# A PSUM bank of its own for gate and lists, and float16 expert products from the third set on

## The chip, the cores and the metric

The kernel runs on one core of a Trainium2 chip. TensorE multiplies, VectorE, ScalarE and GpSimd work on tiles in SBUF and PSUM, SyncE (SP) issues most DMAs. The metric is the device time of one launch in microseconds; lower is better. TensorE's operands may be float32 read in a reduced form (fp32r) or float16; a product of full accuracy is made of three such products of high and low parts.

## The reference

Two layers follow each other. The first is a filter in the frequency domain over 8 batches of 2496 tokens with 256 channels, the second a mixture of 8 experts with two chosen per token, over all 19968 tokens:

```
X = rfft(x, axis=1);  y = irfft(X * (filt_r + 1j * filt_i), n=2496, axis=1)
x = y.reshape(19968, 256)
noisy = x @ w_gate + log1p(exp(x @ w_noise)) * noise
top2 = two largest of noisy per token;  g = softmax over these two
out[token] += g[k] * (relu(x[token] @ w1[e]) @ w2[e])     # for both k, e = top2[k]
```

w1 is 8 x 256 x 1024, w2 is 8 x 1024 x 256.

## The kernel before, in words

**Two streams in one program.** The transform of batch after batch (`fft_stream`) is cut into small steps: `s1`, `kg1`, `kg2`, `t3`, `i2` are matrix products with small tables, each followed by an eviction from PSUM by ScalarE or VectorE. The expert (`expert`) is a generator that yields after each piece of a token block. `run` draws transform steps between the expert's pieces, as many as `PACE` asks for. Each engine executes its instructions in the order in which they stand.

**Sets and blocks.** When a batch is transformed and its tokens are assigned, the tokens that fill whole blocks of 512 for one expert become the next set. Sets 0 and 1 have 2 and 10 blocks, sets 2 and 3 six each, sets 4 to 7 ten each; singles and half blocks follow. In the code `ready` is the set's number plus one. A block takes 13 expert steps: 8 hidden tiles f (relu of x by w1: six products of 512 columns each), one step for the next block's front, and 4 output tiles (h by w2: 24 products of 256 columns each). A hidden tile is evicted twice, by ScalarE (`hh`, line 1371) and VectorE (`hl`, line 1372); an output tile is scaled by the gate on ScalarE (line 1398) and added to the output by an indirect DMA of GpSimd.

**Number formats.** Where `ready >= HALF` the weights, x and the hidden tiles are split into float16 pairs, scaled by powers of two (`wsplit`, `turn`, `pair`); before that they are fp32r pairs. The scales need the largest values. `wscales` finds them in 88 steps (`NPREP`): 64 loads of 256 KB of weights (`wp`, line 598), each squared with accumulation on ScalarE (line 603), then 12 loads of y with a maximum on VectorE (line 620), and two `powers` steps. A load is issued two steps ahead of its square. `run` spreads the steps so that they end after `READY` expert steps:

```
while not self.scaled and state["due"] * READY < NPREP * state["y"]:
    state["due"] += 1
    next(self.preps)
```

For later batches `xscale` makes a scale from the maxima that `i2` leaves in `ymax`.

**Gate and lists.** At the end of a batch's transform `logit_sum`, `logits` and `gating` put the logits into a PSUM tile `lg`; `gate` is a chain of small VectorE instructions to the two chosen experts (`oh`), their weights (`dense`) and, with the products `rk`, each token's place in its expert's list. `slots` (`sl`, `st`) makes the table of blocks. `route` writes the lists: one-hot tiles `oc` on VectorE (lines 1060 to 1062), products `ra` (line 1065), a transpose, and an indirect DMA. `i2` copies `dense` behind the rows of the odd half (line 549) before these go to DRAM.

**PSUM.** Eight banks: "hps" 2 (hidden), "yps" 2 (outputs), "xps" 1 and "fps" 3. After the start all tiles that are asked for by `ps` come from "fps": the transform's and those of gate, slots and lists. Every third hidden tile uses "xps" from set 1 on (`by_dma`), and "yps" in set 0.

Of the kernel before, what the change touches and what calls it, by code (L numbers as in the profile page):

```python
# [24 lines left out]
NG = 22  # L25
# [110 lines left out]
RAW = 3  # L136
HALF = 5
EVERY = 3
# [7 lines left out]
TINY = 2.0 ** -60  # L146
EARLY = {"q1": "hps", "q2": "hps", "q5": "yps", "q6": "yps", "u1": "xps", "u3": "yps"}
BANKS = {"hps": 2, "yps": 2, "xps": 1, "fps": 3}

# [3 lines left out]
class Moe:  # L153
# [40 lines left out]
    def setup(self):  # L194
# [36 lines left out]
        self.tab = cp.tile([1, 2, SW], F32, name="tab")  # L231
        self.ymax = cp.tile([128, 2 * NB, 6], F32, name="ymax")
        self.xm = cp.tile([128, 1], F32, name="xm")
        self.wmax = cp.tile([128, 2 * E], F32, name="wmax")
# [78 lines left out]
    def ps(self, nm):  # L313

        tag = self.banks.get(nm, "fps") if self.early else "fps"
        return self.PS.tile([128, 512], F32, tag=tag, name=nm, bufs=BANKS[tag])

# [205 lines left out]
    def i2(self, n, g0):  # L523
        nc, P, h = self.nc, self.P, n % 2
        Dh, Dl = self.cD
        th, tl = self.t3t.pop((n, g0))
        k = min(4, NG - g0)
        m = 128 * k
        p = self.ps("q6")
        if tl is None:  # L530
            nc.tensor.matmul(p[:RP, :m], self.rD, th[:120, :m], start=True, stop=True)
        else:
            nc.tensor.matmul(p[:RP, :m], Dh, th[:120, :m], start=True, stop=False)
            nc.tensor.matmul(p[:RP, :m], Dh, tl[:120, :m], start=False, stop=False)
            nc.tensor.matmul(p[:RP, :m], Dl, th[:120, :m], start=False, stop=True)  # L535
        w = 128 + E * h
        if n == 0:
            yt = P.tile([RP, 4, 128], F32, name="yt", tag=("mxl0", "mxh1", "mxl1")[g0 // 4 % 3], bufs=1)
        else:
            yt = P.tile([RP, 4, 128 + E], F32, name="yt", bufs=2)  # L540
        e = nc.scalar.copy(yt.bitcast(U16)[:, :k, :256].rearrange("p g (two d) -> p g two d", two=2),  # L541
                       p.bitcast(U16)[:RP, :2 * m].rearrange("p (g d two) -> p g two d", g=k, two=2))
        if n == 2:
            self.yev.append(e)
        if n >= 2 * FIRSTS:
            nc.vector.tensor_reduce(self.ymax[:RP, n, g0 // 4:g0 // 4 + 1], yt.bitcast(U16)[:, :k, 128:256].bitcast(BF16),
                                    axis=AX.XY, op=ALU.max, apply_absolute_value=True)
        if h:
            nc.scalar.copy(yt[:, :k, 128:], self.dense[:, g0:g0 + k])
        y = self.y[BLK + n // 2 * ROWS:BLK + (n // 2 + 1) * ROWS].rearrange("(p g) d -> p g d", p=RP)  # L550
        nc.sync.dma_start(y[:, g0:g0 + k, h * 128:h * 128 + w], yt.bitcast(I32)[:, :k, :w])
# [26 lines left out]
    def xscale(self, bt):  # L578

        nc = self.nc  # L580
        if not self.known:
            self.owed.append(bt)
            return
        nc.vector.tensor_reduce(self.xm, self.ymax[:, :2 * bt + 2], axis=AX.XY, op=ALU.max)
        q = yield from self.powers(self.xm, 1, TX)
        t = self.xs[bt + 1] = self.cp.tile([128, 2], F32, name=f"xs{bt}")
        nc.vector.tensor_copy(t, q[:, :, 0])
        yield
# [270 lines left out]
    def gate(self, bt, lgp):  # L859
# [11 lines left out]
        u, w, l, z = A[:, 17:], B[:, 16:], t("gl"), t("gz")  # L871
        nc.scalar.activation(u, lg[:, :, 8:16], AF.Exp)

        v.tensor_scalar_add(w, u, 1.0)
# [9 lines left out]
        nz = t("gz")  # L884
        v.tensor_add(nz, l, lg[:, :, 0:8])
        keyb = self.key[:RP].unsqueeze(1).to_broadcast(sh)
# [5 lines left out]
        for i in range(2):  # L892
            mi, ci = t(f"m{i}", [RP, NG]), t(f"c{i}", [RP, NG])
            oi = P.tile(sh, F32, name=f"oh{i}", tag=("gl", "oh1")[i], bufs=1)
# [28 lines left out]
        v.tensor_mul(nz, oh[1], bc(e2))  # L923
        v.tensor_add(self.dense, self.dense, nz)
        yield None
        q = self.ps("rk")
        nc.tensor.matmul(q[:RP, 0:8], self.tri[:RP, :RP], rs, start=True, stop=True)
        nc.tensor.matmul(q[:, 8:16], self.ones[:RP, :128], rs, start=True, stop=True)
        nc.tensor.matmul(q[:E, 16:17], rs, self.ones[:RP, 0:1], start=True, stop=True)


# [4 lines left out]
        v.scalar_tensor_tensor(mm, hb, -float(LR), self.base, op0=ALU.mult, op1=ALU.add)  # L936
        v.scalar_tensor_tensor(rw, mm, float(LR - 1), q[:, 8:16], op0=ALU.add, op1=ALU.add)
        v.tensor_single_scalar(rw, rw, 7, op=ALU.arith_shift_right)
# [6 lines left out]
        v.scalar_tensor_tensor(mm, beg, float(LR), mm, op0=ALU.mult, op1=ALU.add)  # L945
        rb = t("rb", [RP, E])
        v.tensor_add(rb, q[:RP, 0:8], mm[:RP])
        v.tensor_add(src, src, rb.unsqueeze(1).to_broadcast(sh))
# [21 lines left out]
        v.tensor_scalar_add(rf, ri, -float(BLK + bt * ROWS + ROWS // 2))  # L970
        v.tensor_add(self.base, self.base, q[:, 8:16])
        v.tensor_add(self.cnt, self.cnt, q[:E, 16:17])
        yield hi, lo, row, rf
# [59 lines left out]
    def route(self, bt, hi, lo, row, rf):  # L1033
# [10 lines left out]
        lr, tv = self.half[:RP, :4 * LR].rearrange("p (l j) -> p l j", j=4), self.half[:RP, 4 * LR:]  # L1044
        for g0 in range(0, NG, 4):
            q = self.ps("ra")[:, :HR]
            for g in range(g0, min(g0 + 4, NG), 2):
                t = P.tile([128, 1024], F16, name="oc", tag=("xh", "xl", "b")[g // 2 % 3], bufs=1)


                ol, vv = t[:RP, 0:4 * LR], t[:RP, 4 * LR:4 * LR + 4 * HR]
                if bt < 2:
                    ol, vv = (a.rearrange("p (l j) -> p l j", j=4) for a in (ol, vv))
                else:
                    ol, vv = (a.rearrange("p (j l) -> p l j", j=4) for a in (ol, vv))

                def w(a):
                    return a if bt < 2 else a.rearrange("p l j -> p j l")

                v.tensor_tensor(w(vv), w(lr[:, :HR]), w(bc(hi[:, g:g + 2], HR)), op=ALU.is_equal)  # L1060
                v.tensor_mul(w(vv), w(vv), w(tv[:, 2 * g:2 * g + 4].unsqueeze(1).to_broadcast([RP, HR, 4])))
                v.tensor_tensor(w(ol), w(lr), w(bc(lo[:, g:g + 2], LR)), op=ALU.is_equal)
                for j in range(4):
                    n = RP if g + j // 2 < NG - 1 else QA
                    nc.tensor.matmul(q, ol[:n, :, j], vv[:n, :, j], start=(g == g0 and j == 0), stop=(j == 3 and g + 2 >= min(g0 + 4, NG)))
            if g0 == 0:
# [8 lines left out]

        o = P.tile([HR, LR], F32, name="ro", **(dict(tag="th", bufs=3) if bt < 2 else dict(tag="ut1", bufs=1)))
        v.tensor_single_scalar(o, q, 0.0, op=ALU.not_equal)
# [256 lines left out]
    def expert(self, parts, may, fill=None):  # L1334
# [5 lines left out]
        while self.ahead:  # L1340
# [10 lines left out]
            if not self.ahead or self.ahead[0][3] or sum(len(a[2][0]) for a in self.ahead) < 4:  # L1351
                self.fetch(may)
            third = ("xps", 1) if self.by_dma(ent) else ("yps", 2)
            hh = []
# [172 lines left out]
```

## Time and profile before

| what | before |
|---|---|
| median of 3 runs | 2177.8 us (2176.26 to 2184.05) |
| the profiled execution | 2164.38 us, span 2162.5 us |
| granted TensorE clock, mean | 0.991 |
| TensorE busy | 2095.9 us, 14517 matmuls |
| VectorE busy | 1466.3 us |
| ScalarE busy | 1286.1 us |
| DMA | 428.48 MB, 198 GB/s over the span |

The span is the time from the first to the last instruction of one profiled execution. A busy matmul is a pipelined one: the durations of neighbours overlap, and what a product costs is the step from its start to the next start. Set 0 begins its first block near 142 us, set 1 at 221, set 2 at 517, set 3 at 693, set 4 at 868.

### The profile page before, as it was taken

The numbers are of one execution on the slowest core, as the hardware profiler recorded it, in microseconds if no ns is written. First come the engines' busy times: TensorE is split into PE (matmuls) and PEld (weight loads), VectorE is DVE, ScalarE is ACT, GpSimd is POOL, SyncE is SP. The second block draws the span as 40 slices with busy tenths as digits, with TensorE's granted clock in tenths as the row PEclk, the third lists the DMA queues.
The fourth block names the chain that finished last, engine by engine and source line by source line (L and its number), as shares of the span: only waits on it lengthen the run. The fifth ranks groups of instructions, "written<-read, shape, count | busy, mean of one in ns | idle before, by whom it ended". The sixth has DMA issues, their size and how long they took to land. (4 is left out here: it accounts for less than half of the span.)

```text
span 2162.5 us, 42794 instructions
## 1 busy us (share of the span) xinstructions
PE 2095.9 (97%) x14517; PEld 1595.5 (74%) x14517; DVE 1466.3 (68%) x3221; ACT 1286.1 (59%) x2505; POOL 1029.2 (48%) x946
## 2 busy tenths in 40 slices
PE   8779999999999999999999999999999999999997
PEld 6447988888888888766766676666666666667886
DVE  5866779877978886678665986589666664333443
ACT  6666866786577446656664565555566564333443
POOL 4233334434544344445444453555655665654563
PEclk9989999999999999999999999999999999999999
DMA  9588989999999775767766687666889999869997
GB/s 255 165 259 223 222 223 215 252 228 228 223 214 233 161 156 137 178 150 183 155 156 131 152 182 165 146 121 132 233 210 240 240 249 234 170 142 229 276 280 175
DMA packets 511673, 428.48 MB, mean 198 GB/s; under 512 B 215679, under 2 KB 397015, under 8 KB 511447
## 3 DMA queue, kind: packets, MB, share of 16 engines
q1 hardware_dynamic: 450135, 341.27, 60.2%
q0 software_dynamic: 61312, 84.40, 23.1%
q8 instruction: 116, 1.90, 0.4%
q14 instruction: 110, 0.90, 0.1%
HBM read 263.92 MB, written 122.03 MB: 178 GB/s over the span
## 5 line engine op out<-in xcount | busy, mean ns | idle before, releaser
L1372 DVE SCALAR_TENSOR_TENSOR hl<-hps,hh 128x512 f16<-128x512 f32 (+3 forms) x712 | 432.4, 623 | 356.6 <-ACT hh L1371 354.7
L1399 POOL DMA_INDIRECT out<-stage,ids x316 | 532.9, 1686 | 270.4 <-ACT stage L1398 167.0
L1158 POOL DMA_INDIRECT stage<-y,ids x316 | 347.9, 1101 | 535.7 <-DMA xt<-stage 433.9
L124 PE MATMUL yps<-w,hh 128*128 128x256 f16 (+1 forms) x2048 | 556.5, 278 | 5.2 <-ACT stage L1398 3.4
L125 PE MATMUL yps<-w,hh 128*128 128x256 f16 (+1 forms) x2048 | 551.2, 277 | 0.0
L126 PE MATMUL yps<-w,hl 128*128 128x256 f16 (+1 forms) x2048 | 541.9, 277 | 1.8 <-DVE hl L1372 1.5
L1371 ACT ACTIVATE hh<-hps 128x512 f16<-128x512 f32 (+3 forms) x712 | 376.7, 550 | 198.9 <-PE hps L126 183.8
L125 PE MATMUL hps<-mxl,w1h 128*128 128x512 f16 (+1 forms) x1024 | 394.4, 386 | 2.2 <-DVE mxl L1246 1.3
L126 PE MATMUL hps<-mxh,w1l 128*128 128x512 f16 (+1 forms) x1024 | 394.0, 386 | 0.0
L124 PE MATMUL hps<-mxh,w1h 128*128 128x512 f16 (+1 forms) x1024 | 385.6, 388 | 5.1 <-DVE hl L1372 5.1
L1398 ACT ACTIVATE stage<-yps,gt 128x256 f32<-128x256 f32 x316 | 143.1, 475 | 329.0 <-PE yps L126 202.0
L124 PEld LDWEIGHTS <-hh 128*128 128x128 f16 x1760 | 172.2, 98 | 52.4 <-issue 6.2
L126 PEld LDWEIGHTS <-hl 128*128 128x128 f16 x1760 | 171.5, 98 | 47.9 <-DVE hl L1372 1.9
L125 PEld LDWEIGHTS <-hh 128*128 128x128 f16 x1760 | 172.2, 98 | 34.2 <-issue 2.6
L124 PEld LDWEIGHTS yps<-w,hh 128*128 128x128 f32 x768 | 145.8, 190 | 12.5 <-ACT stage L1398 2.2
L126 PEld LDWEIGHTS yps<-w,hl 128*128 128x128 f32 x768 | 145.0, 190 | 10.3 <-issue 1.7
L125 PEld LDWEIGHTS yps<-w,hh 128*128 128x128 f32 x768 | 145.4, 191 | 4.6
L126 PEld LDWEIGHTS <-w1l 128*128 128x128 f16 x640 | 62.6, 98 | 71.8 <-issue 1.5
L541 ACT COPY yt<-q 117x1024 uint16<-117x1024 uint16 x96 | 90.9, 947 | 40.7 <-PE q L535 32.1
L1228 DVE COPY stage<-xt 128x1024 uint16<-128x1024 uint16 (+2 forms) x174 | 109.0, 679 | 1.4 <-DMA xt<-stage 1.4
L124 PEld LDWEIGHTS <-w1h 128*128 128x128 f16 x640 | 62.4, 98 | 51.5 <-issue 5.5
L125 PEld LDWEIGHTS <-w1h 128*128 128x128 f16 x640 | 62.6, 98 | 51.1 <-issue 3.0
(286 smaller groups left out, 4024.4 us busy)
## 6 DMA issues: line engine op xcount, KB each, us to landing
stage<-w SPq DMA_DIRECT2D x328, 256.0 KB
x<-x SPq DMA_DIRECT2D x88, 256.0 KB
fd<-c SPq DMA_DIRECT2D x77, 240.0 KB
fi<-wpl SPq DMA_DIRECT2D x18, 1024.0 KB
fx<-fd SPq DMA_DIRECT2D x140, 128.0 KB
out<-z SPq DMA_DIRECT2D x24, 702.0 KB
wp<-w SPq DMA_DIRECT2D x64, 256.0 KB
fr<-w SPq DMA_DIRECT2D x16, 1024.0 KB
```

The lines of the kernel that those rows point to most:

```text
L124: nc.tensor.matmul(o, lh, rh, start=start, stop=False)
L125: nc.tensor.matmul(o, lh, rl, start=False, stop=False)
L126: nc.tensor.matmul(o, ll, rh, start=False, stop=stop)
L541: e = nc.scalar.copy(yt.bitcast(U16)[:, :k, :256].rearrange("p g (two d) -> p g two d", two=2), p.bitcast(U16)[:RP, :2 * m].rearrange("p ( ...
L1158: self.pin(lambda: nc.gpsimd.indirect_dma_start(out=x.bitcast(I32), out_offset=None, in_=self.y[:BLK + ready * ROWS], in_offset=bass.Indir ...
L1228: nc.vector.tensor_copy(xu.rearrange("p (t two) -> p two t", two=2), ent[3][0][:, 2 * kc:2 * kc + 2, :w])
L1371: self.relu = hold(lambda: nc.scalar.activation(h, p, AF.Relu))
L1372: v = hold(lambda: nc.vector.scalar_tensor_tensor(l, p, 0.0, hf[0], op0=ALU.max, op1=ALU.subtract))
L1398: nc.scalar.activation(o, p, AF.Copy, scale=gate[:, t])
L1399: a = nc.gpsimd.indirect_dma_start(out=self.io["out"][:BLK + ready * ROWS], out_offset=bass.IndirectOffsetOnAxis(ap=ids[:, t:t + 1], axis= ...
```

## The change

`HALF` goes from 5 to 3, so sets 2 and 3 work in float16 too, and `READY` follows. The tiles `lg`, `rk`, `sl`, `st` and `ra` come from "xps"; the third hidden tile uses "yps" until the last list is made. `gate` reads the logits into SBUF (`clean`) at once, and `total` and `below` likewise from `rk`. From the third batch on `dense` goes to DRAM in a DMA of its own, and `i2` no longer copies it. `route` makes the one-hot tiles of a group one step ahead of their products, in the buffers "ut0", "ul" and "ut1" and no longer in the transform's "xh", "xl" and "b".

```diff
-HALF = 5
+HALF = 3
...
 READY = 13 * SETS[HALF - 2] - 32
...
+APART = {"lg", "rk", "sl", "st", "ra"}
...
-        tag = self.banks.get(nm, "fps") if self.early else "fps"
+        tag = self.banks.get(nm, "fps") if self.early else "xps" if nm in APART else "fps"
...
-        w = 128 + E * h
+        w = 128 + (E * h if n < 4 else 0)
...
-        if h:
+        if h and n < 4:
             nc.scalar.copy(yt[:, :k, 128:], self.dense[:, g0:g0 + k])
...
+        clean = lg[:, :, 0:8]
+        if bt >= 2:
+            clean = P.tile(sh, F32, name="clean", tag="oh1", bufs=1)
+            nc.scalar.copy(clean, lg[:, :, 0:8])
...
-        v.tensor_add(nz, l, lg[:, :, 0:8])
+        v.tensor_add(nz, l, clean)
...
+        if bt >= 2:
+            y = self.y[BLK + bt * ROWS:BLK + (bt + 1) * ROWS].rearrange("(p g) d -> p g d", p=RP)
+            nc.sync.dma_start(y[:, :, D:], self.dense.bitcast(I32))
...
+        below, total = q[:RP, 0:8], q[:, 8:16]
+        if bt >= 2:
+            below, total = t("rb", [RP, E]), P.tile([128, E], F32, name="total", tag="gd", bufs=1)
+            v.tensor_copy(total, q[:, 8:16])
+            v.tensor_copy(below, q[:RP, 0:8])
+            v.tensor_add(self.cnt, self.cnt, q[:E, 16:17])
...
+        def place(g):
+            nonlocal made
+            if bt < 2:
+                t = P.tile([128, 1024], F16, name="oc", tag=("xh", "xl", "b")[g // 2 % 3], bufs=1)
+            else:
+                t = P.tile([128, 4 * LR + 4 * HR], F16, name="oc", tag=("ut0", "ul", "ut1")[made % 3], bufs=1)
+                made += 1
...
+            else:
+                hot = [place(g) for g in gs]
+                yield
+                q = self.ps("ra")[:, :HR]
+                for g, o in zip(gs, hot):
+                    add(q, g0, g, *o)
...
-            third = ("xps", 1) if self.by_dma(ent) else ("yps", 2)
+            third = ("xps", 1) if self.done_routes == NB - 1 else ("yps", 2)
```

Left out here: `place` holds the three VectorE instructions that stood in `route`, `add` its four products; the tile `ro` uses the buffer "gl" and no longer "ut1"; the scales of x lie in one tile `xst`.

## Rows read from the trace of the kernel before

**Rows 1.** The page, part 1: busy time, share of the span, instructions.

```profile
PE 2095.9 (97%) x14517; PEld 1595.5 (74%) x14517; DVE 1466.3 (68%) x3221; ACT 1286.1 (59%) x2505; POOL 1029.2 (48%) x946
```

**Rows 2.** Stretches: length, busy time of each engine, clock, DMA share, GB/s.

```profile
142.00:221.00 79.00, 71.83 (x404) 55.54 (x403) 55.23 (x160) 50.68 (x99) 23.87 (x22) 0.95 0.85 221
221.00:371.00 150.00, 147.93 (x961) 129.72 (x960) 118.91 (x259) 106.63 (x224) 57.90 (x50) 1.00 0.92 221
371.00:517.00 146.00, 146.00 (x963) 128.83 (x962) 111.59 (x214) 115.02 (x239) 61.40 (x52) 1.00 1.01 239
517.00:693.00 176.00, 172.06 (x1114) 152.31 (x1113) 148.58 (x327) 125.06 (x255) 78.18 (x61) 1.00 0.92 220
```

**Rows 3.** TensorE's waits, 517 to 1597: total us, times, longest.

```profile
PE hps L124 <- DVE hl L1372: 4.7, 6, 1.4
PE yps L124 <- ACT stage L1398: 3.4, 2, 1.8
PE ra L1065 <- DVE oc L1061: 2.2, 3, 1.1
PE q L411 <- DVE tl L520: 1.4, 1, 1.4
```

**Rows 4.** TensorE's timeline, set 3 (fp32r): start us, duration, instruction.

```profile
711.22 0.28 PE L125 MATMUL yps<-w,hh 128*128 128x256 f32 x1
...
712.78 0.28 PE L126 MATMUL yps<-w,hl 128*128 128x256 f32 x1
...
714.70 0.39 PE L125 MATMUL hps<-mxl,w1h 128*128 128x512 f32 x1
...
715.63 0.39 PE L126 MATMUL hps<-mxh,w1l 128*128 128x512 f32 x1
```

**Rows 5.** TensorE's timeline, set 4 (float16).

```profile
941.12 0.27 PE L124 MATMUL yps<-w,hh 128*128 128x256 f16 x1
...
946.25 0.27 PE L126 MATMUL yps<-w,hl 128*128 128x256 f16 x1
...
951.40 0.38 PE L124 MATMUL hps<-mxh,w1h 128*128 128x512 f16 x1
...
952.48 0.38 PE L126 MATMUL hps<-mxh,w1l 128*128 128x512 f16 x1
```

**Rows 6.** Stretches, "mxl" alone: PE, PEld, DVE (its splits), clock, DMA, GB/s.

```profile
517.00:693.00 176.00, 37.91 (x96) 18.08 (x96) 8.16 (x12) 1.00 0.92 220
693.00:868.00 175.00, 38.01 (x96) 18.07 (x96) 7.68 (x12) 1.00 0.72 159
```

**Rows 7.** Groups on TensorE by form: count | busy us, mean ns | idle before.

```profile
L124 PE MATMUL yps<-w,hh 128*128 128x256 f32 x768 | 217.0, 286 | 3.2 <-ACT stage L1398 1.8 <-ACT hh L1371 1.4
...
L124 PE MATMUL hps<-mxh,w1h 128*128 128x512 f32 x384 | 152.5, 402 | 5.1 <-DVE hl L1372 5.1
```

**Rows 8.** Groups on VectorE by form: low part of w1.

```profile
L1204 DVE SCALAR_TENSOR_TENSOR w1l<-stage,sc,w1h 128x512 f16<-128x512 f32 x80 | 59.6, 744 | 52.9 <-ACT w1h L1203 52.4 <-issue 0.4
...
L1323 DVE TENSOR_TENSOR w1l<-stage,w1h 128x512 fp32r<-128x512 f32 x84 | 57.9, 693 | 15.2 <-ACT w1h L1322 15.1
```

**Rows 9.** Line 603 (squares): ns min/median/max, first and last start; idle before.

```profile
L603 ACT ACTIVATE wp<-wp x64: 614/632/695, 175.7 to 630.3; 128x512 f32<-128x512 f32 x64
L603 ACT ACTIVATION_READ_ACCUMULATOR wp<-wp x64: 185/196/263, 176.2 to 630.8; 128x1 f32 x64
...
  DMA wp<-w: 5.9, 3
```

**Rows 10.** Stretches, line 603 alone: ACT busy (two records a square).

```profile
142.00:221.00 79.00, 3.96 (x11) 0.95 0.85 221
221.00:371.00 150.00, 15.21 (x44) 1.00 0.92 221
```

**Rows 11.** ScalarE's timeline near 576 us: start, duration, idle before.

```profile
575.71 0.63 ACT L603 ACTIVATE wp<-wp 128x512 f32<-128x512 f32 x1 [4.10 <-DMA wp<-w]
```

**Rows 12.** SP's own waits over the whole span: total us, times, longest.

```profile
SPq L551 <- ACT yt L549: 68.7, 31, 10.8
```

More of the change, by code (lines that the diff above doesn't have):

```diff
@@ L232, in setup @@
         self.ymax = cp.tile([128, 2 * NB, 6], F32, name="ymax")
+        self.xst = cp.tile([128, NB, 2], F32, name="xst")
         self.xm = cp.tile([128, 1], F32, name="xm")
@@ L585, in xscale @@
         q = yield from self.powers(self.xm, 1, TX)
-        t = self.xs[bt + 1] = self.cp.tile([128, 2], F32, name=f"xs{bt}")
+        t = self.xs[bt + 1] = self.xst[:, bt]
         nc.vector.tensor_copy(t, q[:, :, 0])
@@ L892, in gate @@
         for i in range(2):
-            mi, ci = t(f"m{i}", [RP, NG]), t(f"c{i}", [RP, NG])
+            mi, ci = t(f"m{i}", [RP, NG]), t("c0", [RP, NG])
             oi = P.tile(sh, F32, name=f"oh{i}", tag=("gl", "oh1")[i], bufs=1)
@@ L936, in gate @@
         v.scalar_tensor_tensor(mm, hb, -float(LR), self.base, op0=ALU.mult, op1=ALU.add)
-        v.scalar_tensor_tensor(rw, mm, float(LR - 1), q[:, 8:16], op0=ALU.add, op1=ALU.add)
+        v.scalar_tensor_tensor(rw, mm, float(LR - 1), total, op0=ALU.add, op1=ALU.add)
         v.tensor_single_scalar(rw, rw, 7, op=ALU.arith_shift_right)
@@ L945, in gate @@
         v.scalar_tensor_tensor(mm, beg, float(LR), mm, op0=ALU.mult, op1=ALU.add)
-        rb = t("rb", [RP, E])
-        v.tensor_add(rb, q[:RP, 0:8], mm[:RP])
+        rb = below if bt >= 2 else t("rb", [RP, E])
+        v.tensor_add(rb, below, mm[:RP])
         v.tensor_add(src, src, rb.unsqueeze(1).to_broadcast(sh))
@@ L970, in gate @@
         v.tensor_scalar_add(rf, ri, -float(BLK + bt * ROWS + ROWS // 2))
-        v.tensor_add(self.base, self.base, q[:, 8:16])
-        v.tensor_add(self.cnt, self.cnt, q[:E, 16:17])
+        v.tensor_add(self.base, self.base, total)
+        if bt < 2:
+            v.tensor_add(self.cnt, self.cnt, q[:E, 16:17])
         yield hi, lo, row, rf
@@ L1044, in route @@
         lr, tv = self.half[:RP, :4 * LR].rearrange("p (l j) -> p l j", j=4), self.half[:RP, 4 * LR:]
-        for g0 in range(0, NG, 4):
[L1046 to L1065, printed above, removed]
@@ new lines, in route, with w @@
+        made = 0
+        def place(g):
+            nonlocal made
+            if bt < 2:
+                t = P.tile([128, 1024], F16, name="oc", tag=("xh", "xl", "b")[g // 2 % 3], bufs=1)
+            else:
+                t = P.tile([128, 4 * LR + 4 * HR], F16, name="oc", tag=("ut0", "ul", "ut1")[made % 3], bufs=1)
+                made += 1
+            ol, vv = t[:RP, 0:4 * LR], t[:RP, 4 * LR:4 * LR + 4 * HR]
+            if bt < 2:
+                ol, vv = (a.rearrange("p (l j) -> p l j", j=4) for a in (ol, vv))
+            else:
+                ol, vv = (a.rearrange("p (j l) -> p l j", j=4) for a in (ol, vv))
+            def w(a):
+                return a if bt < 2 else a.rearrange("p l j -> p j l")
+            v.tensor_tensor(w(vv), w(lr[:, :HR]), w(bc(hi[:, g:g + 2], HR)), op=ALU.is_equal)
+            v.tensor_mul(w(vv), w(vv), w(tv[:, 2 * g:2 * g + 4].unsqueeze(1).to_broadcast([RP, HR, 4])))
+            v.tensor_tensor(w(ol), w(lr), w(bc(lo[:, g:g + 2], LR)), op=ALU.is_equal)
+            return ol, vv
@@ new lines, in add @@
+        def add(q, g0, g, ol, vv):
+            for j in range(4):
+                n = RP if g + j // 2 < NG - 1 else QA
+                nc.tensor.matmul(q, ol[:n, :, j], vv[:n, :, j], start=(g == g0 and j == 0), stop=(j == 3 and g + 2 >= min(g0 + 4, NG)))
+        for g0 in range(0, NG, 4):
+            gs = range(g0, min(g0 + 4, NG), 2)
+            if bt < 2:
+                q = self.ps("ra")[:, :HR]
+                for g in gs:
+                    add(q, g0, g, *place(g))
+            else:
+                hot = [place(g) for g in gs]
+                yield
+                q = self.ps("ra")[:, :HR]
+                for g, o in zip(gs, hot):
+                    add(q, g0, g, *o)
@@ L1073, in route @@
         x = x[:HR]
-        o = P.tile([HR, LR], F32, name="ro", **(dict(tag="th", bufs=3) if bt < 2 else dict(tag="ut1", bufs=1)))
+        o = P.tile([HR, LR], F32, name="ro", **(dict(tag="th", bufs=3) if bt < 2 else dict(tag="gl", bufs=1)))
         v.tensor_single_scalar(o, q, 0.0, op=ALU.not_equal)
```

## The prediction, made before the changed kernel ran

> **What bounds the kernel now.** I read the page's busy shares first: TensorE is busy 97% of the span, VectorE 68%, ScalarE 59% [rows 1]. A busy matmul is a pipelined one, so the share alone proves little; the second view was the stretches by set of token blocks. From 221 us on TensorE lacks little: 2.1 us of 221 to 371, nothing of the 146.0 us of 371 to 517, 3.9 us of 517 to 693, at a granted clock of 1.00, that is 2.4 GHz [rows 2]. The reader is to see there that TensorE's idle time does not follow the DMA share or ScalarE's busy time: the stretch with the fullest DMA engines, 1.01, is the one without a gap. The third view was what TensorE waited for from 517 to 1597: of 1080 us the longest entries are 4.7, 3.4, 2.2 and 1.4 us, each behind VectorE or ScalarE [rows 3]. So after the first 221 us the end is set by how fast TensorE gets through its instructions, and a change is worth what it takes off that stream, less what it makes TensorE wait.
>
> **Pace of the products.** The trace has both number formats. A hidden product (512 columns) in fp32r starts 0.93 us after the fourth before it, 232.5 ns each; an output product (256 columns) starts 1.56 us after the thirteenth before it, 120 ns [rows 4]. In float16 the steps are 1.08/5 = 216 ns and 5.13/47 = 109.1 ns [rows 5]. The durations in the grouped view (about 400 and 286 ns) are those of pipelined instructions and no pace.
>
> **The change, part by part.**
>
> *Float16 from the third set.* Only sets 2 and 3 change format: each has 12 splits of x, two for a block, so 6 blocks [rows 6]. By count a block has 48 hidden and 96 output products: the 384 and 768 of one line, three lines, over 24 fp32r blocks [rows 7]. One block gains 48 x 16.5 ns + 96 x 10.9 ns = 1.84 us, twelve gain **22.1 us**. These products run back to back on the bounding engine, so I take all of it. The splits of weights and x are scaled in float16: on VectorE 744 ns and not 693 [rows 8], some 0.05 us for each of ten splits a block in set 2 and six in set 3: 5 us in all. It lies beside TensorE, but set 2 has VectorE busy for 148.6 of 176 us [rows 2]; if that cover is gone the price is those 5 us. I take 1 us lost, ends 0 and 5.
>
> The Trainium skill weighs against this term: by its page "TensorE: Matmul & The Clock Gate", section "Back-to-back issue gap", a warm matmul follows the one before after N/2.4 + 2.5 ns, whatever the number format. That is 216 and 109 ns, which are the float16 steps of this trace; by that page the fp32r products would already run so and the term would be 0. The rows of the two formats differ by 16 and 11 ns, and the rows decide.
>
> *Two more scale steps* (for the inputs of sets 2 and 3), each one transpose and two small products for TensorE, and twelve more scale copies on GpSimd: I take 1 us, below that nothing.
>
> *The weight maxima must be ready earlier.* READY falls from 13 x 24 - 32 = 280 steps to 13 x 12 - 32 = 124, 13 steps a block. 64 loads of 256 KB, each read by a square with accumulation on ScalarE (632 + 196 ns), ran from 175.7 to 630.3 us, one per 7.1 us [rows 9]. There are 88 preparation steps, the squares end at step 66: after 66 x 124/88 = 93 of the expert's steps, 7.15 blocks. Sets 0 and 1 are 12 blocks in 142 to 517 us, 31 us each, so the squares now end near 366 us, one per 3.5 us. By 371 us 55 records, some 28 squares, had run before [rows 10]; 36 more come into this stretch. On ScalarE that is 36 x 0.83 = 30 us onto 157 of 229 us: 82%, where 371 to 517 has 79% without a TensorE gap [rows 2]. On the DMA engines it is 9.4 MB, 41 GB/s more on 221; pro rata to the share of 0.90 that gives 1.06, above the 1.01 seen. Each load is issued two preparation steps ahead of its square, 14 us before and 7 us now; where a load is late, ScalarE stands still and the evictions queue behind the square. Before, 3 of 64 squares stood, 5.9 us in all [rows 9], and one cost TensorE: behind the 4.10 us wait that ended at 575.71 [rows 11] an output product waited 1.8 us for an eviction, the longest of its entry [rows 3]. With half the lead I take three times as many waits, a third of which cost 1.8 us: 3 x 1.8 = **5.4 us** lost. Ends: 0 (as 371 to 517), and every third square at 1.8 us, 21 x 1.8 = 38 us. In set 2 the one event of before goes: 1.8 us back.
>
> *Gate and lists in the bank "xps"; the third hidden product in "yps".* The transform keeps three banks to itself. TensorE's waits in transform matmuls (line 411, 1.4 us) come after the transform's own evictions on VectorE [rows 3], and would still be there: gain 0, end 2 us. The third hidden product of sets 1 to 6 now shares two banks with the outputs. The first output pair takes the bank of f = 2, five hidden tiles of six products, 30 x 0.22 = some 7 us, after it is filled, while its two evictions go on beside them: cost 0; without that cover a block would wait once for an eviction. Gate, rank, slots and lists now share one bank one after another; each is read within a few us and the steps are spread, cost 0.
>
> *Lists.* For sets from the third on, one-hot tiles are made one step before their matmuls, in buffers of their own: the wait of "ra" for "oc", **2.2 us** [rows 3], goes. *Gate weights* leave for DRAM in one DMA of 32-byte pieces per batch, and not with the odd half's rows: 36 ScalarE copies leave and one per batch comes, nothing on the path. On SP's queue the row DMAs had waited 68.7 us in 31 times for that copy [rows 12]; now one issue per batch waits for "dense", and weight and transpose loads queue behind it. That trades many waits for one: 0, with an end of 3 us either way.
>
> The sum: -22.1 + 1 + 1 + 5.4 - 1.8 - 2.2 = **-18.7 us**. The profiled execution took 2164.4 us (span 2162.5), giving 2145.7; the runs shown have a median of 2177.8 us, 13 above it, so 2159.1 there.
>
> **Rivals.**
> *The squares stall ScalarE more often.* For it: half the lead, and a DMA demand above anything seen; against it: 371 to 517 at share 1.01. Without the preparation term the sum is -24.1 us. At 8 to 19 stalls of 1.8 us the gain is inside half a per cent; 13 give 2177.
> *The same stall, from 20 on, makes it slower.* One mechanism: in sets 0 and 1 a square waits for its load and TensorE for the eviction behind it. From 20 of 64 the cost (36 us) passes the gain by more than half a per cent; 25 stalls give -24.1 + 45 = +21, 2199 us. The slower side ends here.
> *VectorE becomes the bound of sets 2 and 3.* 148.6 + 3 us of work in 176 - 11 us is 92%. If half of the format's gain stays behind VectorE, -18.7 + 11 = -8: 2170 us. Against it: the longest entry of TensorE's waits for VectorE's "hl" is 4.7 us in 1080 us [rows 3].
> *The formats' pace is no property of the format.* Then the term of 22.1 us is 0 and the sum +3.4, 2181 us. The rule of the Trainium skill above would have it so; the rows speak plainly against it.
>
> **How the numbers follow.** Half a per cent, 10.9 us, is about what a measurement of this kernel can tell from no change. Forecast 0.61 (faster by more than that), stalls of the middle size 0.15, slower 0.13, VectorE 0.09, pace 0.02. So faster 0.61, within 0.26, slower 0.13. The likeliest is 2159 us, its own range 2147 (no stall and the small terms at their better ends, -30 us) to 2167. To leave out no more than two in ten the range reaches over the cases within half a per cent as far as 16 stalls, +5 us: 2147 to 2183.
>
> **What would show it.** In the trace after: sets 2 and 3 step at 216 and 109 ns; squares between 175 and about 370 us; "ra" no longer waits for "oc"; TensorE's idle time from 142 to 517 grows by about 5 us and the stretch of twelve blocks behind it is some 26 us shorter. I am wrong if ScalarE's wait for "wp" in that stretch is tens of us and outputs wait for evictions, if waits for "hl" grow in sets 2 and 3, or if the scales come so late that set 2 begins with a gap.

## The result: slower by one per cent, and the profile after

| what | before | after |
|---|---|---|
| median of 4 runs each, side by side | 2177.0 us (2175.1 to 2184.1) | 2199.2 us (2197.0 to 2202.7) |
| ratio, 95% interval | | 1.0101 (1.0080 to 1.0122) |
| the profiled execution | 2164.4 us | 2197.0 us |
| mean granted clock | 0.991 | 0.986 |

The forecast was 2159 us (2147 to 2183); the kernel is 22 us slower than before and 40 us above the forecast. The two profiled executions differ by 32.6 us, since that of before lies 13 us below its median and that of after 2 us below: of what the traces differ by, some 10 us belong to that one execution of before.

The page of after, busy time, share of the span and instructions [rows 1]:

```profile
PE 2101.6 (96%) x14527; PEld 1525.0 (69%) x14527; DVE 1466.2 (67%) x3253; ACT 1289.3 (59%) x2475; POOL 1057.0 (48%) x967
```

The stretches of after (columns as in [rows 2]: length; PE, PEld, DVE, ACT, POOL busy; clock, DMA share, GB/s):

```profile
142.00:221.00 79.00, 72.22 (x415) 57.33 (x414) 56.93 (x166) 55.93 (x116) 25.70 (x23) 0.95 0.86 241
221.00:371.00 150.00, 140.68 (x854) 119.10 (x853) 104.56 (x202) 121.58 (x263) 48.70 (x42) 0.98 1.00 256
371.00:517.00 146.00, 132.13 (x847) 110.03 (x846) 121.41 (x292) 93.40 (x190) 55.14 (x40) 1.00 0.86 207
517.00:693.00 176.00, 167.48 (x1108) 126.40 (x1107) 146.72 (x347) 119.01 (x217) 93.08 (x71) 0.97 0.84 189
```

TensorE now lacks 9.3 us of 221 to 371 (before 2.1), 13.9 of 371 to 517 (before nothing) and 8.5 of the next stretch (before 3.9), at a granted clock below 1.00 in two of them. No engine is full there: VectorE has 226 of 296 us, ScalarE 215. The stretch without a gap before, 371 to 517 at a DMA share of 1.01, now has the most gaps at 0.86.

The same by set, where a set runs from the first split of x of its first block (`mxl` on VectorE, 1 to 4 us ahead of its first hidden product) to that of the next set. Set 1 of both kernels, one stretch each (before, then after):

```profile
219.50:514.60 295.10, 293.03 (x1915) 257.68 (x1914) 229.65 (x472) 220.75 (x462) 119.45 (x101) 1.00 0.96 229
```

```profile
215.70:580.60 364.90, 335.27 (x2093) 284.50 (x2092) 284.20 (x658) 256.84 (x529) 143.21 (x108) 0.98 0.91 224
```

Set 1 is **69.8 us** longer. In it 178 more products were executed (2093 against 1915), nearly all of transform and lists, and TensorE stood 29.6 us and not 2.1. Sets 2 to 6 give back 38.5 us, what stands ahead of set 1 gives 3.8, and from set 7 on 5.2 are lost: 69.8 - 38.5 - 3.8 + 5.2 = 32.7 us, the difference of the spans. I also split sets 1 to 6 by kind, each product counted at its usual step in the trace of before: the expert's products fall by 21.8 us, the others rise by 1.2 (much the same work), and what is left, standing and running slowly, rises from 48.2 to 100.2 us, 50.8 of these 52.0 in set 1, where the other products take 81.5 us and not 62.6. This split is an estimate, good to some 5 us: with the products counted by time windows, what is left grows by 45.8 us in set 1 and by 18.0 in set 2, and falls by 13.5 in the sets behind.

What ScalarE waited for DMAs in set 1, before, then after (total us, times, longest):

```profile
ACT w1h L1322 <- DMA stage<-w: 7.4, 9, 1.8
```

```profile
ACT wp L605 <- DMA wp<-w: 39.9, 17, 7.7
ACT w1h L1358 <- DMA stage<-w: 18.4, 7, 6.0
```

Two kinds of load are late: those of the preparation (`wp`) and the weights that the products themselves need (`stage`). ScalarE's timeline at one of the second kind, and TensorE's behind it (start, duration, idle before in brackets):

```profile
537.85 0.62 ACT L1358 CAST w1h<-stage 128x512 fp32r<-128x512 f32 x1 [6.04 <-DMA stage<-w]
```

```profile
541.13 0.58 PE L124 MATMUL yps<-w,hh 128*128 128x256 f32 x1 [4.98 <-ACT hh L1407]
```

ScalarE stood 6.04 us until a piece of w1 had landed at 537.85; the evictions queued behind it, and an output product started 4.98 us late. No load of the preparation was in its way, since the last of them (12 of y, first and last start) was issued at 482.4 us:

```profile
L617 SPq DMA_DIRECT2D wp<-y x12: 334/348/574, 418.3 to 482.4; - x12
```

So not all of set 1's loss is the preparation's. The squares, line 605 (ns min/median/max, first and last start, idle before):

```profile
L605 ACT ACTIVATE wp<-wp x64: 615/633/696, 166.9 to 421.9; 128x512 f32<-128x512 f32 x64
...
  DMA wp<-w: 46.8, 21
```

They end at 422 us (forecast 366, before 630 [rows 9]), and 21 stood for 46.8 us (before 3 and 5.9). The float16 steps in set 2, hidden and output products:

```profile
599.28 0.38 PE L124 MATMUL hps<-mxh,w1h 128*128 128x512 f16 x1
...
600.36 0.38 PE L126 MATMUL hps<-mxh,w1l 128*128 128x512 f16 x1
...
613.82 0.27 PE L126 MATMUL yps<-w,hl 128*128 128x256 f16 x1
...
615.02 0.27 PE L125 MATMUL yps<-w,hh 128*128 128x256 f16 x1
```

1.08 us for five steps and 1.20 for eleven: 216 and 109 ns, as [rows 5]. The format's gain is there.

### The profile page after: what moved, and what is told of

Its sections match the earlier page's. It is cut to its first block, busy times and chain, and to the rows that moved or that the text cites. A ratio compares the mean times of both kernels' runs of the same rounds, so it can differ in the third digit from the quotient of the medians.

```text
span 2195.2 us, 42919 instructions
## 1 busy us (share of the span) xinstructions
PE 2101.6 (96%) x14527; PEld 1525.0 (69%) x14527; DVE 1466.2 (67%) x3253; ACT 1289.3 (59%) x2475; POOL 1057.0 (48%) x967
## 5 line engine op out<-in xcount | busy, mean ns | idle before, releaser
L1194 POOL DMA_INDIRECT stage<-y,ids x316 | 358.3, 1134 | 527.4 <-DMA xt<-stage 455.8
L124 PEld LDWEIGHTS <-hh 128*128 128x128 f16 x2144 | 210.0, 98 | 60.9 <-issue 10.3
L126 PEld LDWEIGHTS <-hl 128*128 128x128 f16 x2144 | 209.4, 98 | 51.9 <-issue 3.1
L125 PEld LDWEIGHTS <-hh 128*128 128x128 f16 x2144 | 210.0, 98 | 33.9 <-issue 0.9
L1240 DVE SCALAR_TENSOR_TENSOR w1l<-stage,sc,w1h 128x512 f16<-128x512 f32 x116 | 86.3, 744 | 93.5 <-ACT w1h L1239 49.8
L126 PEld LDWEIGHTS <-w1l 128*128 128x128 f16 x832 | 81.7, 98 | 95.9 <-issue 1.7
L124 PEld LDWEIGHTS <-w1h 128*128 128x128 f16 x832 | 81.7, 98 | 76.4 <-issue 11.2
L125 PEld LDWEIGHTS <-w1h 128*128 128x128 f16 x832 | 81.7, 98 | 75.8 <-issue 10.9
L1239 ACT ACTIVATE w1h<-stage,sc 128x512 f16<-128x512 f32 x116 | 83.4, 719 | 67.6 <-PE hps L125 39.7
L1144 POOL CAST ids<-lt 128x4 int32<-128x4 f32 (+3 forms) x66 | 19.4, 294 | 210.5 <-DMA lt<-lst 209.2
L1240 DVE SCALAR_TENSOR_TENSOR mxl<-stage,xst,mxh 128x512 f16<-128x512 f32 (+2 forms) x154 | 103.8, 674 | 13.2 <-ACT mxh L1239 11.2
L1239 ACT ACTIVATE mxh<-stage,xst 128x512 f16<-128x512 f32 (+2 forms) x154 | 101.9, 662 | 17.1 <-PE hps L126 13.7
```

The source lines that it names most:

```text
L124: nc.tensor.matmul(o, lh, rh, start=start, stop=False)
L125: nc.tensor.matmul(o, lh, rl, start=False, stop=False)
L126: nc.tensor.matmul(o, ll, rh, start=False, stop=stop)
L1144: nc.gpsimd.tensor_copy(ids, t)
L1194: self.pin(lambda: nc.gpsimd.indirect_dma_start(out=x.bitcast(I32), out_offset=None, in_=self.y[:BLK + ready * ROWS], in_offset=bass.Indir ...
L1239: self.nc.scalar.activation(h, x, AF.Copy, scale=s)
```

## The experiments

Three theories. **P**: the preparation, 64 loads and squares pressed into sets 0 and 1, makes ScalarE and so TensorE wait. **B**: gate and lists in the bank "xps" cost by themselves. **T**: with a bank and list buffers of their own, gate and lists no longer hold back the transform, so that the order of instructions that is fixed when the program is built draws transform tiles forward into set 1, where they compete with everything else. For T I counted, in the compiled order of TensorE, the transform's tiles (`q`, of all its steps) between the starts of sets 1 and 2: 87 before, 110 after. In this count nothing was timed.

All runs in one table; ratio to the kernel before on the same chip. The three columns on the right are from one profiled execution each: set 1's length, TensorE's idle time in it, and the last block before the first float16 set.

| kernel | ratio (95%) | tiles in set 1 | set 1 us | idle us | last block us |
|---|---|---|---|---|---|
| before | 1 | 87 | 295.1 | 2.1 | 32.8 |
| after | 1.0101 (1.0080, 1.0122) | 110 | 364.9 | 29.6 | 31.6 |
| x1_banks_alone | 1.0088 (1.0060, 1.0116) | 130 | 352.1 | 16.5 | 26.1 |
| x2_half3_alone | 1.0213 (1.0185, 1.0241) | 109 | 413.5 | 69.5 | 105.2 |
| x3_no_maxima | 0.9995 (0.9972, 1.0017) | 111 | 342.1 | 16.9 | 33.0 |
| x4_half4 | 1.0014 (0.9996, 1.0032) | 122 | 345.2 | 15.9 | 26.6 |
| x5_bank_old_lists | 1.0062 (1.0044, 1.0081) | 91 | 307.9 | 5.0 | 36.2 |
| x6_banks_slow_pace | 1.0146 (1.0107, 1.0185) | 87 | 311.2 | 8.2 | 60.0 |
| x7_half3_slow_pace | 1.0032 (1.0014, 1.0050) | 88 | 328.1 | 19.7 | 30.9 |
| x8_no_maxima_slow_pace | 1.0052 (1.0038, 1.0067) | 83 | 300.1 | 6.1 | 28.3 |
| l_loads | 1.0096 (1.0071, 1.0121) | 110 | 373.3 | 40.0 | 32.4 |
| m_squares | 0.9932 (0.9912, 0.9953) | 110 | 336.3 | 12.1 | 35.6 |
| b_half4 | 1.0168 (1.0143, 1.0194) | 87 | 303.3 | 7.7 | 104.9 |
| g_nobank4 | 1.0143 (1.0121, 1.0165) | 88 | 308.9 | 9.5 | 89.5 |
| q_act_queue | 1.0004 (0.9986, 1.0023) | 109 | 346.7 | 19.3 | 37.2 |
| q_quarter | 0.9985 (0.9968, 1.0001) | 109 | 347.0 | 17.9 | 37.3 |
| p125_4 | 1.0073 (1.0048, 1.0098) | 88 | 322.4 | 15.9 | 33.8 |
| q_act_p125 | 0.9974 (0.9960, 0.9989) | 88 | 321.6 | 19.5 | 30.1 |
| q_act_queue4 | 1.0008 (0.9993, 1.0023) | 122 | 354.7 | 21.0 | 26.3 |
| before_act | 1.0033 (1.0018, 1.0048) | 88 | 302.4 | 3.3 | 32.8 |

**One part alone.** x1 is the changed kernel with float16 back at the fifth set, x2 the kernel before with float16 from the third.

```diff
x1 (from after)          x2 (from before)
-HALF = 3                -HALF = 5
+HALF = 5                +HALF = 3
```

> The changed kernel with HALF = 5 again: banks, buffers, the separate DMA of the gate weights and the one-step-ahead one-hot tiles are there, the float16 sets and the earlier weight maxima are not. Theory P (the earlier preparation costs the time: squares on ScalarE wait for their loads in sets 0 and 1): within 5 us of the kernel before, 2172 to 2180 us, and set 1 near 295 us. Theory B (the new places for gate, lists and third hidden tile cost it): 2190 to 2200 us, set 1 near 350 us.

> The kernel before with HALF = 3 and nothing else of the change. Theory P: 2190 to 2205 us, set 1 longer by 50 to 70 us than before, sets 2 and 3 shorter. Theory B: the products' gain shows, 2150 to 2160 us.

The two do not add, and neither theory alone has both: x1 lies near B's range, x2 above P's. The bank and list edits alone cost 0.9%, the formats alone 2.1%, both together 1.0%. In x2 the last block before the first float16 set lasted 105.2 us, and one cause stands out (TensorE's waits in that block, 527.0 to 632.2):

```profile
PE ra L1065 <- DVE oc L1061: 14.7, 3, 8.2
PE rk L927 <- DVE rs L911: 12.3, 1, 12.3
```

Gate and lists run there in one piece on VectorE, with TensorE empty. I found the same in b_half4 and g_nobank4 (below), in none of the kernels where the lists have a bank of their own, and in none with float16 from the fifth set (the 60.0 us of x6 hold 9.0 us of idle TensorE). x2 also has 109 tiles in set 1, without the bank: of its products of transform and lists, 234 stand in that last block (before 73), where the changed kernel has them spread over the set. So with float16 from the third set the number of tiles does not tell what the bank does; with the fifth it does, 87 before and 130 in x1.

**Without the preparation, and float16 one set later.** x3 leaves out the 64 loads and squares (the weight maximum is a constant, so scales differ); x4 is the changed kernel with `HALF = 4`, the preparation spread over 202 steps.

```diff
-        yield from pairs(load, top, 8 * E)
+        v.memset(self.wmax, 0.25)
+        for _ in range(8 * E + 2):
+            yield
```

> The changed kernel without the 64 weight loads and their squares: the weights' largest values are a constant, the preparation steps stay empty. Theory P: the some 50 us that TensorE loses in set 1 go, 2140 to 2155 us. Theory B: only the DMA and ScalarE time of the squares is saved beside TensorE, 2185 to 2197 us.

> The changed kernel with HALF = 4: READY is 202 steps, set 3 alone gets float16 early (a gain of 11 us), a square every 5 to 6 us. Theory P: the stalls fall steeply with the rate, 2165 to 2182 us. Theory B: 2195 to 2205 us, as half of the format's gain is missing.

Without loads and squares the whole loss of 1% goes, TensorE's idle time in set 1 from 29.6 to 16.9 us. P holds as to the amount, yet 16.9 us stay (before 2.1): P is not all. x4, with a gain of half the format and the preparation slower, comes out level, as P had it.

**The transform's place.** x5 is x1 with the one-hot tiles back in the old buffers and in one step; x6, x7 and x8 slow the transform in set 1: `PACE[1]` 110 in x1, 125 in the changed kernel, 110 in x3.

```diff
-PACE = {0: 110, 1: 200, 2: 60}
+PACE = {0: 110, 1: 110, 2: 60}
```

> HALF = 5, gate and lists in the bank xps and the third hidden tile in yps, but the one-hot tiles again in the transform's buffers and made beside their products. In the compiled order of TensorE 91 transform tiles then stand between the starts of sets 1 and 2, against 87 in the kernel before and 130 with the list buffers too. Theory T (with bank and buffers both free nothing holds the transform back; the compile-time scheduler pulls it into set 1, where the other engines are full, and TensorE stalls there): as the kernel before, within 5 us, and TensorE loses under 12 us in set 1. Theory B (the new bank, or the third hidden tile among the outputs, itself costs the time): 2185 to 2195 us.

> All of the new banks and buffers with HALF = 5, and PACE of set 1 lowered from 200 to 110 transform steps: 87 transform tiles stand in set 1 of the compiled order and not 130. Theory T: TensorE's loss in set 1 falls from 33 us to about 10, 2165 to 2178 us. Theory B: still 2185 to 2195 us.

> The changed kernel with PACE of set 1 at 125: 88 transform tiles in set 1 and not 110. Theory T with theory P for the rest: the some 34 us lost without the squares go, the some 20 us that the squares add stay: 2160 to 2180 us. Theory P alone (the squares explain the loss, wherever the transform stands): 2190 to 2200 us.

> The changed kernel without the 64 loads and squares (the weights' largest values are a constant) and with PACE of set 1 at 110, 83 transform tiles in set 1. Theory T with P: both causes are gone and the products' gain of 22 us shows, 2140 to 2155 us. If something else in the change costs time in set 1: 2160 us or more.

x5 says that the bank alone does not draw the transform forward: 91 tiles, set 1 at 307.9 us; with the buffers free as well (x1) 130 tiles and 352.1. For set 1 alone, x3, x7, x8 and after give a square of four, if the two slow paces (88 and 83 tiles) are taken as one; in the split by kind, what is left over the products is 13.1 us without preparation and with the slow transform, 34.1 with the fast one, 37.5 with preparation and the slow one, 56.8 with both. So preparation costs some 23 us in set 1 and the transform drawn forward some 20, each good to 5 us, and the two add. They also stand apart in time. Set 1 up to 422 us, where the squares of the changed kernel end, and behind it (after, x7, x3, x8):

```profile
215.70:422.00 206.30, 190.85 (x1180) 162.20 (x1178) 146.86 (x314) 159.73 (x348) 71.05 (x58) 0.98 0.98 250
422.00:580.60 158.60, 144.41 (x915) 122.30 (x914) 137.34 (x345) 97.11 (x182) 72.17 (x50) 0.97 0.83 190
```

```profile
217.00:422.00 205.00, 188.30 (x1157) 160.93 (x1156) 147.93 (x327) 156.83 (x344) 70.74 (x60) 0.98 0.97 244
422.00:545.10 123.10, 120.09 (x778) 104.05 (x778) 97.01 (x201) 74.78 (x143) 56.83 (x47) 0.99 0.85 197
```

```profile
212.90:422.00 209.10, 203.48 (x1310) 177.76 (x1310) 172.59 (x354) 147.28 (x275) 76.73 (x64) 0.99 0.82 199
422.00:555.00 133.00, 121.69 (x747) 102.59 (x746) 110.06 (x290) 76.83 (x146) 56.53 (x44) 0.96 0.87 194
```

```profile
216.90:422.00 205.10, 202.02 (x1315) 177.33 (x1315) 165.07 (x366) 132.87 (x251) 93.97 (x71) 0.99 0.82 195
422.00:517.00 95.00, 91.98 (x564) 81.35 (x564) 74.53 (x139) 61.00 (x112) 36.51 (x35) 0.98 0.83 200
```

While the loads run, TensorE stands 15.5 and 16.7 us with them and 5.6 and 3.1 without; behind them it stands 14.2 and 11.3 us with the fast transform and 3.0 with the slow one, loads or not. For the whole time T holds less well. x5 takes 13 us more than before (1.0062) where T gave at most 5, so a cost of the bank itself (B) is not excluded. x6 is slower than x1, with a block of 60.0 us before the fifth set, and x8 than x3, with 210.5 us for set 2 and not 191.3. Tiles that leave set 1 seem to be paid for elsewhere; why is not shown.

**Loads or squares.** l_loads keeps the loads and leaves out the squares; m_squares squares a resident tile and loads nothing. In both the maximum is a constant.

```diff
 l_loads: -  nc.scalar.activation(t, t, AF.Square, accum_out=...)
 m_squares: -  nc.sync.dma_start(t, io["w1" if i < 4 * E else "w2"][i // 4 % E, i % 4])
            -  nc.scalar.activation(t, t, AF.Square, accum_out=...)
            +  nc.scalar.activation(t, f32v(self.hl[:, :512]), AF.Square, accum_out=...)
```

> The changed kernel with the 64 weight loads of the preparation kept and their 64 squares left out; the weight maximum is a constant, so the outputs' scales differ. Its compiled order has 110 transform tiles between the starts of the second and third sets, as the changed kernel. If the loads themselves cost (DMA share, the weight loads behind them), the time lost in that set stays near the 57 us of the changed kernel and the run takes about 2195 us beside 2172. If the cost lies in ScalarE standing at a square, the time lost is near the 34 us of the run without loads and squares, the run takes about 2170 to 2176 us, and TensorE's waits for evictions in that set are those of that run.

> The changed kernel with the 64 squares kept, each over a tile that lies in SBUF, and their loads left out; the weight maximum is a constant, so the outputs' scales differ. 110 transform tiles in the second set. If ScalarE's time for the squares (64 x 0.83 = 53 us) is what costs, the set loses about 57 us as in the changed kernel and the run takes about 2195 us beside 2172. If it is the wait of a square for its load that costs, a square never waits, the set loses about 34 us and the run takes 2170 to 2176 us. If both this run and the one with loads alone stay near 2172, only the two together cost, which is the wait. If each takes some 2183, half the price lies in either.

This is the clearest result: loads alone 1.0096, squares alone 0.9932, neither 0.9995 (x3). Standing at a square, the form in which I had put P, is not needed. ScalarE's waits in set 1 of l_loads, then of m_squares:

```profile
ACT w1h L1356 <- DMA stage<-w: 48.9, 15, 10.9
```

```profile
ACT w1h L1357 <- DMA stage<-w: 17.6, 11, 3.2
```

With no square to stand at, ScalarE stood nearly as long for the products' weights, whose loads come late. Not all of it is the preparation's: x3, without any of its loads, has 28.3 us of this wait in 13 times, so some 20 us are. SP waited 35.2 us in 25 times at the preparation's loads for a buffer whose former load was still under way, and the weight loads stood behind it in its queue; that this is what made them late is argued and not shown.

```profile
SPq L600 <- DMA wp<-w: 35.2, 25, 5.2
```

**Fewer float16 sets in the kernel before.** b_half4 is the kernel before with `HALF = 4`; g_nobank4 the changed one with `HALF = 4` and all of gate and lists back in "fps".

> The kernel before with float16 from the fourth set on, and no other edit: gate and lists in the transform's bank and the lists' old buffers. The six blocks of one set change format, a gain of 6 x 1.84 = 11 us. The compiled order keeps 87 transform tiles in the second set, as the kernel before. The maxima are due 202 steps in and not 280. By the theory that preparation costs only where it is pressed into the second set and stands ScalarE still, the squares come one per 5 us, a price of 2 to 8 us: 2163 to 2170 us where the kernel before takes 2172, ratio 0.996 to 0.999. By the theory that the stalls grow in step with the rate of loads (23 us for the change from 280 to 124 steps, so about half for 202), the gain is eaten: ratio 1.000.

> The changed kernel with float16 from the fourth set on and gate and lists back in the transform's bank (the third hidden tile back where it was); the lists' new buffers, their step ahead and the one store of the gate weights a batch stay. The compiled order has 88 transform tiles in the second set. By the theory that bank and list buffers cost only where both are free and the transform moves into the second set, this run does as the kernel before with float16 from the fourth set, less up to 2 us for the lists' wait: ratio 0.995 to 0.999. If the list buffers, the extra step or the one store cost by themselves, it is slower than that kernel by the size of that cost.

Both missed by far, 1.0168 and 1.0143 where 0.995 to 1.000 was expected. The block before the fourth set lasts 104.9 us in b_half4, and about its end VectorE is busy for 24.9 of 27.1 us and TensorE for 9.0, at half the clock:

```profile
674.20:779.10 104.90, 75.69 (x448) 62.24 (x446) 71.37 (x197) 54.78 (x102) 29.96 (x29) 0.81 0.64 151
...
755.90:783.00 27.10, 8.99 (x40) 5.21 (x40) 24.89 (x100) 5.81 (x9) 1.53 (x3) 0.50 0.15 43
```

So with float16 one or two sets earlier and lists in the transform's bank, the batch's last tiles and its list come in one piece just ahead of the first float16 set; with the lists' own bank they do not (x4, 26.6 us for that block). That the compiled order does this because the set's inputs wait for the scale is argued and not shown. The list buffers and the one store of `dense` cost nothing that shows: g_nobank4 has them and is not slower than b_half4.

**Queue or bytes.** q_act_queue lets ScalarE issue the loads that it reads, q_quarter loads and squares a quarter of each piece (the maximum is a constant), and p125_4 is the changed kernel with `HALF = 4` and `PACE[1] = 125`.

```diff
 q_act_queue:
-            with self.after(self.spw):
-                nc.sync.dma_start(t, io["w1" if i < 4 * E else "w2"][i // 4 % E, i % 4])
+            nc.scalar.dma_start(t, io["w1" if i < 4 * E else "w2"][i // 4 % E, i % 4])
 q_quarter:
+                nc.sync.dma_start(t[:, :128], io["w1" if i < 4 * E else "w2"][i // 4 % E, i % 4, :, :128])
```

> The changed kernel with the 64 loads of the preparation issued by ScalarE, which reads them, and not by SP. A load then never waits for a square of another engine, and SP's queue of weight loads has none of them in it; bytes, buffers and due times are the same. 109 transform tiles in the second set. If the cost is SP's queue, the second set loses about 30 to 35 us as without loads, and the run takes 2165 to 2172 us beside 2172. If it is the bytes on full DMA engines, the set loses about 57 us, the DMA share from 221 to 371 us is 1.00 again and the run takes some 2195 us.

> The changed kernel with each of the 64 loads cut to a quarter of its columns (64 KB and not 256) and squared over that quarter; the weight maximum is a constant, so the outputs' scales differ. Number, place and buffers of the loads are the same. 109 transform tiles in the second set. If the bytes cost (12.6 MB fewer), the set loses about 30 to 35 us and the run takes 2165 to 2172 us beside 2172. If the places in SP's queue cost, SP waits for squares as before, the set loses about 57 us and the run takes some 2195 us.

> The changed kernel with float16 from the fourth set on and the transform of the second set paced at 125 and not 200. 88 transform tiles in the second set. By the theory that the loads and the transform drawn into the second set compete for the same DMA engines, both are thinner here: the format gains 11 us, the set loses no more than the 13 to 15 us of the runs with few transform tiles and slow loads, and the run takes 2160 to 2168 us beside 2172, ratio 0.995 to 0.998. If the scales of the fourth set come late, as in the kernel before with float16 from the fourth set, the last block of the third set is some 100 us long and the run takes over 2190 us.

Both of the first two give back about 1%, so neither explanation stands alone. Out of SP's queue the loads ran with the DMA engines fuller than in this stretch of before or after (q_act_queue, 221 to 371 us):

```profile
221.00:371.00 150.00, 141.89 (x892) 123.95 (x893) 109.82 (x222) 125.52 (x272) 55.55 (x46) 0.98 1.04 269
```

TensorE still lacks 8.1 us there (after 9.3, x3 2.3); what q_act_queue saves lies behind, from 371 to 600 us, 10.1 us of idle time and not 21.6. In SP's queue with a quarter of the bytes, SP's wait for a square at the loads falls from 24.0 to 10.7 us in set 1, though squares still stood 28.2 us. But before had 28.2 us of the same wait of SP in its set 1, and TensorE stood 2.1 us, so that wait is not the price by itself. What the runs show is that shortening the loads or moving them helps; by what path, and how the price divides between queue and bytes, stays open. p125_4 missed: 1.0073. Its sets 2 and 3 lose 19 and 17 us by the split, for which I have no cause.

**Both measures together.** q_act_p125 is q_act_queue with `PACE[1] = 125`, q_act_queue4 is q_act_queue with `HALF = 4`, before_act is the kernel before with the loads on ScalarE alone.

> The changed kernel with the 64 loads issued by ScalarE and the transform of the second set paced at 125 and not 200 (88 transform tiles there). If the two causes add, as in the four runs with and without loads and pace, the set loses some 13 to 20 us where the changed kernel loses 57 and the run with ScalarE's loads 41, and the run takes 2150 to 2160 us beside 2172, ratio 0.990 to 0.995. If the transform that is moved out of the set costs as much later (as it did without loads: 45 us in the third set), the ratio stays at 0.998 to 1.004.

> The changed kernel with the 64 loads issued by ScalarE and float16 from the fourth set on (122 transform tiles in the second set, the loads over 202 steps). With SP's loads this kernel had ratio 1.0014. By the queue theory it gains less than the 22 us that the same edit gave with the loads in 124 steps, in step with their rate some 10 us: ratio 0.996 to 0.998. If the loads at this rate cost nothing, the ratio stays at 1.000 to 1.002.

> The kernel before with its 64 loads issued by ScalarE and not by SP; float16 from the fifth set, banks and lists as before, 88 transform tiles in the second set. At one load per 7.1 us they cost that kernel the 1.8 us behind one late load: ratio 0.998 to 1.000 if the queue costs only where the loads are dense. If SP's queue costs it more than the waits of TensorE show, the ratio is 0.995 to 0.998, and the gain of the other kernel is not the format's.

q_act_p125 is the one complete version that beats both kernels: 0.9974 (0.9960, 0.9989), some 6 us, no more than half of what I expected of it; its set 1 still has 19.5 us of idle time, now in many gaps of under 3 us. q_act_queue4 is level with x4 (1.0008 and 1.0014): over 202 steps the move of the loads shows nothing. The moved loads alone do not do it: before_act is slower than before, 1.0033, though its set 1 lacks only 3.3 us. That is also a measure of how far a mere change of order moves this kernel. So is m_squares, which does more work than x3 and is 0.6% faster. From differences below that between kernels whose order differs I draw no cause, and that holds for the 0.26% of q_act_p125 too.

## Why the prediction was wrong

**The format's term, -22.1 us: right.** The steps were 216 and 109 ns and the split gives 21.8 us. The rival that doubted the pace falls: in these traces fp32r and float16 steps differ by 16 and 11 ns. In the Trainium skill's "TensorE: Matmul & The Clock Gate", section "Back-to-back issue gap", the formula of the gap, given there for an isolated matmul, has no number format in it; that it holds whatever the format was my reading. The float16 steps agree with it, the fp32r steps do not.

**VectorE's splits, scale steps, list wait: right or too small to see.** TensorE's waits from 517 to 1597 have no "ra" in them any more (before 2.2 us [rows 3]). The wait for "hl", which I had named as a sign of being wrong, grew from 4.7 to 5.8 us, its longest from 1.4 to 3.7:

```profile
PE yps L124 <- ACT hh L1407: 8.5, 2, 5.0
PE hps L124 <- DVE hl L1408: 5.8, 3, 3.7
```

It grew for another reason than the splits. Ahead of the longest, which ended at 734.81 us, VectorE stood behind ScalarE, and ScalarE behind a late piece of w1:

```profile
732.34 0.72 ACT L1239 ACTIVATE w1h<-stage,sc 128x512 f16<-128x512 f32 x1 [7.01 <-DMA stage<-w]
```

```profile
733.09 0.77 DVE L1240 SCALAR_TENSOR_TENSOR w1l<-stage,sc,w1h 128x512 f16<-128x512 f32 x1 [7.14 <-ACT w1h L1239]
```

**"The weight maxima must be ready earlier", 5.4 us: the step that failed.** The price in set 1 is some 23 us, and x3, without it, gives back as much of the whole time (0.9995 and not 1.0101). Two things were wrong in it. I expected nine waits, three of which reach TensorE; there were 21, of 46.8 us. And I priced ScalarE's work and its waits alone, where the loads did the harm, also to other loads: squares without loads cost nothing (0.9932), loads without squares as much as both (1.0096). I had worked out a DMA demand of 1.06 for this stretch and let it pass because 371 to 517 had 1.01 without a gap; but that stretch had 20 of these loads, and after had 36 in 221 to 371, with no more products of transform and lists beside them (256, there 285). The rival "The same stall, from 20 on" gave 2199 us for 25 stalls. Its time is the measured one and its count near the 21 seen, but that is luck: l_loads has no square to stand at and is as slow, and about half of what set 1 loses has another cause.

**"Gate and lists in the bank xps: gain 0, cost 0": failed too.** I looked for a wait of TensorE that the bank would take away and found 1.4 us. Alone the edits of bank and lists cost 0.9% (x1, some 18 us). What they change is the order: with float16 from the fifth set 43 more tiles stand in set 1 than before, and in the changed kernel, whose tiles are spread over the set, a slower transform takes some 20 us of standing and slow running out of it (after and x7). That this is the whole price of the edits is not shown (x5, x6, x8). Under the earlier float16 the same edit is also worth something that I did not see: without it the block before the first float16 set takes 90 to 105 us. The forecast added terms to each other that depend on each other.

**Covers.** By the forecast TensorE's idle time from 142 to 517 was to grow by about 5 us; it grew from 9.2 to 30.0. The stretch of twelve blocks behind was to be 26 us shorter; sets 2 and 3 are 12.6 us shorter (353.2 before, 340.6 after), set 2 itself 13.8 longer, with the late weights shown above.

## What to carry to other kernels

Where the order of instructions is built ahead, an edit that frees a buffer moves other work forward; count what moves, and where to, before it is priced at nothing. Price a preparation by its loads, their size and the queue in which they stand, and not only by the busy time of the engine that reads them: here 64 squares were free and 64 loads cost about one per cent. And measure the two halves of a change alone before adding their terms: 1.0088 and 1.0213 made 1.0101.

## What the hardware showed unasked

A wait of TensorE can cost more than itself. In the 4.98 us without work before 541.13 the granted clock fell to 0.50, the lower level, and stayed there for some 10 us (stretches of after: before, behind, and later):

```profile
528.00:538.00 10.00, 7.48 (x42) 5.95 (x40) 4.94 (x13) 3.96 (x8) 7.37 (x7) 1.00 1.04 281
539.00:549.00 10.00, 7.87 (x26) 6.59 (x27) 9.93 (x24) 8.42 (x16) 0.24 (x1) 0.50 0.64 148
549.00:580.00 31.00, 30.51 (x213) 27.43 (x211) 27.32 (x95) 16.59 (x30) 24.01 (x14) 1.00 0.74 151
```

Between 220 and 2150 us the trace of before has no such stretch; that of after has five, 30.7 us in all, which at half speed is at most some 15 us on top of the waits themselves. Not every wait had one: behind the 3.07 us that ended at 383.62 the clock stayed at 1.00. None of the forecast's stalls had this price.
